# The head flags' load moved from the head of SyncE's queue to behind the first weight gates

## The chip, the cores and the metric

The kernel runs on one core of a Trainium2 chip. The metric is the device time of one execution in microseconds. In the profile PE is TensorE, DVE is VectorE, ACT is ScalarE, POOL is GpSimd and SP is SyncE.

## The reference

Attention with four batches, eight heads, 768 positions and a head size of 64, then a feed-forward layer whose hidden value is the largest of three products:

```
scores = q @ k.T / 8                                   # per batch and head
mask   = causal                     where is_retrieval[head]
         causal & (first 4 keys | last 64 keys)        otherwise
x      = softmax(where(mask, scores, -1e9)) @ v        # -> (3072 rows, 512)
h      = max(x @ w1, x @ w2, x @ w3)                   # 512 -> 768
out    = h @ w_out                                     # 768 -> 512, float32
```

`is_retrieval` holds eight 64-bit flags, 64 bytes as eight pairs of 32-bit words. In the inputs heads 0, 2 and 6 are retrieval heads.

## The kernel before

The kernel is written for a guess of the flags (`GUESS`), and reads the real flags only to test the guess. The flags are loaded into the tile `ir32` (on one partition, 16 words); `compare_flags` (the word `flags` of the order, on POOL) turns them into one number, and a branch at the end runs a general version if the guess was wrong.

All work stands in one order written out by hand, the string `PROGRAM`, whose words are looked up in the table `do`. Each word adds instructions to the queues of its engines, and each engine works through its own queue in that order. What concerns the change is batch 0, whose keys, queries and values are loaded in two halves of 384 positions. The heads are taken as four pairs, `PAIRS`: pair 0 is heads 0 and 2, pair 1 heads 1 and 3, pair 2 heads 4 and 6, pair 3 heads 5 and 7. The loads of half 0 are named here k0 to k3 (tile `ks`), q0 to q3 (tile `qs`), each 192 KB, and va and vb (tile `vs`), the values of heads 0 to 3 and 4 to 7, 384 KB each. The loads of half 1 that follow are k4 to k7 and q4 to q7.

- `load_first` (L310) calls `load_pairs` (L198), one transfer per pair for the keys and one for the queries, at L206. In half 0 all keys go through SP and all queries through ACT (`sc`); in half 1 both go through SP (`ss`).
- Ahead of the order stand k0, q0, k1, q1 and, at L317, the flags on SP. Then `hl 0 2 2 sc` loads k2, k3, q2, q3, and `load_v 0 0 0 4 s` and `load_v 0 0 4 4 s` (L298) load va and vb on SP.
- `cast` (L220) casts a pair to 16 bits, `turnp` transposes it on PE (L238) and copies it out of PSUM to `KQ` (L241). The second line of the order has `turnp 0 0 ad, cast 0 3 pa, ... s0 0 1 1`, and the third `s0 0 0 0, ... turnp 0 3 da, turnp 0 2 da`: pair 3 is cast on POOL (k3) and ACT (q3), and ACT's later work, two exponentials (L638) and the copies of `KQ`, stands behind the cast of q3 in ACT's queue. PE's transposes of pairs 3 and 2, in this order, stand ahead of all later scores (L602, L617).
- `gs i` is a gate: a copy of four bytes of weight matrix i to a scrap tile (`gates`, L286), issued by SP, which must wait for the weights. It keeps SP's later loads back. `w 0`, `w 1` and `w 2` load the weights on POOL (L401).

The queues are also tied together by the transfers' semaphores. In the built program each transfer that SP or ACT issues takes the next of eight semaphores in turn, in one sequence over both queues, and waits until the transfer eight places earlier has landed. The sequence begins q0, k0, q1, k1, flags, k2, k3, q2, va, q3, vb. So va waits for q0, q3 for k0, vb for q1, k4 for k1, and the next for the flags. The order between the two queues is the build's own estimate of when each engine gets to the transfer; within a queue it is the order of the program.

Of the kernel before, what the change touches and what calls it, by code (L numbers as in the profile page):

```python
# [11 lines left out]
INT32 = mybir.dt.int32  # L12
# [141 lines left out]
def fast(ctx, tc, keep, q, k, v, is_retrieval, n_sink, window, moe_w1, moe_w2, moe_w3, moe_w_out, w_t, woutt, out):  # L154
    nc = tc.nc
# [127 lines left out]
    def gate(engine, x):  # L283
        dst = gates[:, next(n_gate)]
        if engine is nc.sync:
            engine.dma_start(out=dst, in_=x)  # L286
        else:
            engine.tensor_copy(out=dst, in_=x)
# [25 lines left out]
    load_first(0, 0, 1)  # L314
    load_first(0, 1, 1)
    ir32 = keep.tile([1, 2 * H], INT32, name="ir32")
    nc.sync.dma_start(out=ir32, in_=is_retrieval.bitcast(INT32).unsqueeze(0))  # L317

    zero = consts.tile([P, 512], FP16, name="zero")
    nc.vector.memset(zero, 0.0)  # L320
# [3 lines left out]
    def idle_work(n):  # L324
# [11 lines left out]
        out=kb[:, 2:4], in_=kb[:, 2:4], compare_op=ALU.is_ge, fill=0.0,  # L336
# [3 lines left out]
        out=kb[:, 3], in_=kb[:, 3], compare_op=ALU.is_gt, fill=0.0,  # L340
# [3 lines left out]
        out=kb[:, 1:5:3], in_=kb[:, 1:5:3], compare_op=ALU.is_gt, fill=0.0,  # L344
# [7 lines left out]
        out=every3, in_=every3, compare_op=ALU.not_equal, fill=1.0,  # L352
# [4 lines left out]
    if n_sink > 0:  # L357
# [4 lines left out]
        out=far, in0=kb[:, 0:5], scalar1=FAR, scalar2=-FAR, op0=ALU.mult, op1=ALU.add  # L362
# [74 lines left out]
    def hidden(b, half, wi, ni, op=None):  # L437
        yy = psum(b, half)
        for ks in range(KS):
            nc.tensor.matmul(  # L440
                yy[:, 0:HALF],
                w_t[wi][:, ks, ni * P : (ni + 1) * P],
                xT[b, half, ks].rearrange("p a t -> p (a t)"),
                start=(ks == 0), stop=(ks == KS - 1),
            )
        if wi == 0:
            acc[b, half, ni] = accp.tile([P, HALF], FP16, tag="acc", name="acc")
            op(out=acc[b, half, ni], in_=yy[:, 0:HALF])  # L448
            return
        if wi == 2:  # L450
            hT[b, half, ni] = htp.tile([P, HALF], FP16, tag=f"hT{ni}", name=f"hT{ni}")
        nc.vector.tensor_tensor(  # L452
            out=acc[b, half, ni] if wi == 1 else hT[b, half, ni],
            in0=yy[:, 0:HALF], in1=acc[b, half, ni], op=ALU.max,
        )
# [65 lines left out]
    def prep_x(b, half, heads, what, op):  # L521
        by_row = b == 0 and half in sorted_halves
        vs = staged_v[b, half] if not by_row else va[0][:, :, half * HB : (half + 1) * HB, 0:D]
        dst = vx[b % 2]
        hs = slice(*map(int, heads.split(":")))
        which = list(range(*hs.indices(H)))
        xs_ = slice(near.index(which[0]), near.index(which[-1]) + 1)
        n = len(which)
        assert near[xs_] == which
        if what == "r":  # L530
            s0 = 2 * half
            k0 = (1, 0)[half]
            op(out=dst[64:P, xs_, s0 : s0 + 2, 0:D], in_=vs[64:P, hs, k0 : k0 + 2])
        else:
            op(
                out=dst[0:64, xs_, :, 0:D],
                in_=vs[0:64, hs, 0:1].to_broadcast([64, n, 4, D]),
            )
# [7 lines left out]
    kx = [[consts.tile([P, 4, P, 2], FP16, name=f"kx{j}{quad}") for quad in range(2)] for j in range(2)]  # L546
# [30 lines left out]
    def far_keys(b, quad, op):  # L577
        src, dst = KQs[b, quad][:, 0], kx[b % 2][quad]
        op(
            out=dst[:, :, 64:P].rearrange("p n c two -> p n (c two)"),  # L580
            in_=src.rearrange("p (n c) two -> p n (c two)", c=P)[:, 1:5, P : 2 * P],
        )
        if n_sink > 0:
            op(
                out=dst[:, :, 0:n_sink].rearrange("p n c two -> p n (c two)"),
                in_=src[:, 0:n_sink].rearrange("p c two -> p (c two)").unsqueeze(1)
                .to_broadcast([P, 4, 2 * n_sink]),
            )
# [54 lines left out]
    def first_masks(hp, u, r, engine):  # L643
        f = "SR"[GUESS[PAIRS[hp][r % 2]]]
        c, pattern = FIRST_KEEP[f, u]
        mask(pts[0, 1, hp, u], r % 2, 1 if r < 2 else 2, c, P, pattern, engine)
# [161 lines left out]
    def reduce_one(out, in_):  # L808
# [9 lines left out]
        k0=lambda hp, u, r, e: first_masks(int(hp), int(u), int(r), engines[e]),  # L818
        s=lambda b, s: scores(int(b), int(s)),
        k=lambda b, s, xy, i, e: masks(int(b), int(s), xy, int(i), engines[e]),  # L820
        f=lambda b, half, wi, ni, *e: hidden(int(b), int(half), int(wi), int(ni), *[ops[x] for x in e]),
# [5 lines left out]
        y=lambda b, half, hs, what, e: prep_x(int(b), int(half), hs, what, ops[e]),  # L827
# [11 lines left out]
        kx0=lambda half, hp, e: far_keys_first(int(half), int(hp), ops[e]),  # L839
        kx=lambda b, quad, e: far_keys(int(b), int(quad), ops[e]),  # L840
        flags=compare_flags,
        check=check_sums,
        verdict=verdict,
        gs=lambda wi: gate(nc.sync, (w_t + [woutt])[int(wi)][0:1, 0, 0:2]),
# [15 lines left out]
def kernel(  # L860
    tc: tile.TileContext,
    q: bass.AP,
    k: bass.AP,
    v: bass.AP,
    is_retrieval: bass.AP,
    n_sink: int,
    window: int,
    moe_w1: bass.AP,
    moe_w2: bass.AP,
    moe_w3: bass.AP,  # L870
    moe_w_out: bass.AP,
    out: bass.AP,
):
    nc = tc.nc
    B, H, S, D = q.shape
    DF, DM = moe_w1.shape[1], out.shape[1]
    with ExitStack() as ctx:
        keep = ctx.enter_context(tc.tile_pool(name="keep", bufs=1))
        w_t = [keep.tile([128, H * D // 128, DF], FP16, name=f"w{wi}t") for wi in range(3)]
        woutt = keep.tile([128, DF // 128, DM], FP16, name="woutt")  # L880
        xs_dram = tc.dram_tile([B * H, S, D], FP16, name="xs_dram")
        n = fast(
            tc, keep, q, k, v, is_retrieval, int(n_sink), int(window),
            moe_w1, moe_w2, moe_w3, moe_w_out, w_t, woutt, out,
        )
        with tc.If(n > 0, preferred_fallthrough_block=True, label="last"):
            general(tc, nc, q, k, v, is_retrieval, int(n_sink), int(window), w_t, woutt, out, xs_dram)
# [164 lines left out]
```

## Time and profile before

| | us |
|---|---|
| time, median of 3 runs | 188.04 (187.54 to 188.54) |
| time of the profiled execution | 187.23 |
| span of its instructions | 185.7 |
| PE busy | 178.3 (96%) |
| DVE busy | 144.7 (78%) |
| ACT busy | 99.4 (54%) |
| POOL busy | 82.8 (45%) |

The span is the time from the first to the last instruction of the profiled execution; 1.5 us of its own time lie around it. Times in views count from the start of the span. A row of the order in time has start, duration, engine, line of the kernel, operation, output and input tile, count, and in brackets the idle time before it with what ended it. An engine's name with a q, such as SPq or ACTq, is its queue of instructions that are not computation; the rows used here are the issue of transfers, not their movement.

### The profile page before, as it was taken

What the parts mean: (1) busy time and instruction counts of PE and PEld (TensorE: products, weight loads), DVE (VectorE), ACT (ScalarE), POOL (GpSimd) and SP (SyncE); (2) the same over time, 40 slices, a digit from 0 to 9 for tenths busy, and PEclk for the clock granted to TensorE, in tenths of its full rate; (3) what the DMA queues carried; (4) which work ended last, traced back from release to release, by engine and by line L of the source; (5) the groups of instructions that cost most, each with busy time, mean ns of one, the idle gap of its engine ahead of it and who ended that gap; (6) DMA issues with size and microseconds to landing.
All of it is one profiled execution on the core that took longest, in us unless ns stands there. A gap on an engine that the chain in (4) does not pass through costs nothing.

```text
span 185.7 us, 4756 instructions
## 1 busy us (share of the span) xinstructions
PE 178.3 (96%) x1863; PEld 105.8 (57%) x1863; DVE 144.7 (78%) x308; ACT 99.4 (54%) x161; POOL 82.8 (45%) x142
## 2 busy tenths in 40 slices
PE   6889999999999999999999999999999999999992
PEld 2455646566656456755555556655755575555551
DVE  3659998989899978888979899755883699474553
ACT  3399998378956648687096336664446301311110
POOL 7498998809793990299057002126313400000000
PEclk9999999999999999999999999999999999999999
DMA  5999999999899999449593301321132013401404
GB/s 166 320 326 287 214 209 210 211 236 216 166 148 158 201 223 201 110 105 218 142 264 84 114 0 56 67 81 56 28 68 109 0 60 64 139 2 56 165 16 166
DMA packets 43009, 26.30 MB, mean 142 GB/s; under 512 B 29798, under 2 KB 38502, under 8 KB 42982
## 3 DMA queue, kind: packets, MB, share of 16 engines
q1 hardware_dynamic: 37558, 17.24, 35.7%
q0 software_dynamic: 4192, 7.87, 23.6%
q10 hardware_dynamic: 1232, 0.85, 1.5%
q8 instruction: 15, 0.25, 0.5%
q14 instruction: 12, 0.10, 0.2%
HBM read 25.17 MB, written 6.29 MB: 169 GB/s over the span
## 4 chain that ended last, share of the span: by engine, by line
PE 85%; DVE 7%; DMA 4%; ACT 2%; issue 0%; DVEq 0%; ACTq 0%
PE yy L440 47%; PE yy L465 15%; PE oacc L726 8%; PE st L683 7%; PE yst L440 3%; DMA qs<-in_q_dram 2%; DVE KQ L241 2%; DMA ks<-in_k_dram 2%; PE yst L465 1%; DVE KQ L275 1%; ACT pt L638 1%; DVE x L733 1%; DVE vx L809 1%; PE st L617 1%; PE vb L514 1%; PE tr L749 1%
## 5 line engine op out<-in xcount | busy, mean ns | idle before, releaser
L380 POOL TENSOR_TENSOR pt<-pt,kb 128x512 f16<-128x512 f16 (+5 forms) x53 | 48.3, 932 | 59.1 <-ACT pt L700 50.2
L700 ACT ACTIVATE pt<-st 128x1024 f16<-128x1024 f32 (+2 forms) x51 | 43.5, 908 | 25.2 <-PE st L683 24.8
L440 PE MATMUL yy<-xT,w2t 128*128 128x384 f16 x184 | 36.2, 326 | 0.0
L440 PE MATMUL yy<-xT,w0t 128*128 128x384 f16 x180 | 34.6, 326 | 0.0
L440 PE MATMUL yy<-xT,w1t 128*128 128x384 f16 x176 | 34.2, 326 | 0.0
L465 PE MATMUL yy<-woutt,hT 128*128 128x512 f16 (+1 forms) x138 | 31.4, 372 | 0.0
L452 DVE TENSOR_TENSOR hT<-yy,acc 128x384 f16<-128x384 f32 x46 | 25.2, 555 | 5.0 <-PE yy L440 3.3
L452 DVE TENSOR_TENSOR acc<-yy,acc 128x384 f16<-128x384 f32 x44 | 23.9, 554 | 5.6 <-PE yy L440 4.2
L275 DVE STREAM_TRANSPOSE KQ<-kq 128x384 f32<-128x384 f32 x24 | 25.3, 1130 | 0.7 <-DMA kq<-in_k_dram 0.7
L440 PEld LDWEIGHTS <-w0t 128*128 128x128 f16 x192 | 18.1, 98 | 12.5 <-issue 0.4
L448 ACT CAST acc<-yy 128x384 f16<-128x384 f32 x27 | 12.9, 492 | 22.6 <-PE yy L440 20.0
L440 PEld LDWEIGHTS <-w1t 128*128 128x128 f16 x192 | 17.8, 98 | 11.9 <-issue 0.6
L440 PEld LDWEIGHTS <-w2t 128*128 128x128 f16 x192 | 17.7, 98 | 11.8 <-issue 0.2
L465 PEld LDWEIGHTS <-hT 128*128 128x128 f16 x150 | 14.4, 98 | 15.3
L726 PEld LDWEIGHTS <-pt 128*128 128x128 f16 x472 | 17.2, 97 | 3.5 <-issue 0.4
L474 ACT COPY ot<-yy 128x512 f32<-128x512 f32 (+1 forms) x14 | 7.9, 566 | 21.0 <-PE yy L465 19.3
L726 PE MATMUL oacc<-va,pt 128*128 128x65 f16 x392 | 18.6, 193 | 0.2 <-DVE pt L380 0.2
L733 DVE TENSOR_TENSOR x<-oacc,sums 128x384 f16<-128x384 f32 x32 | 17.8, 557 | 1.1
L638 ACT ACTIVATE pt<-st 128x1024 f16<-128x1024 f32 (+5 forms) x22 | 15.5, 769 | 0.4 <-PE st L617 0.2
L683 PE MATMUL st<-KQ 32*128 32x128 f16 (+2 forms) x342 | 14.9, 257 | 0.0
L380 DVE TENSOR_TENSOR pt<-pt,kb 128x256 f16<-128x256 f16 (+4 forms) x31 | 12.2, 400 | 2.1 <-ACT pt L700 2.1
L448 DVE CAST acc<-yy 128x384 f16<-128x384 f32 x18 | 10.0, 558 | 3.4 <-PE yy L440 2.9
(119 smaller groups left out, 191.2 us busy)
## 6 DMA issues: line engine op xcount, KB each, us to landing
out_dram<-ot SPq DMA_DIRECT2D x23, 256.0 KB, 2.0
vs<-in_v_dram SPq DMA_DIRECT2D x18, 256.0 KB, 4.9
ks<-in_k_dram SPq DMA_DIRECT2D x8, 192.0 KB, 3.5
kq<-in_k_dram POOLq DMA_DIRECT2D x3, 384.0 KB, 7.5
kq<-in_q_dram POOLq DMA_DIRECT2D x3, 384.0 KB, 9.1
kq<-in_k_dram POOLq DMA_DIRECT2D x3, 288.0 KB, 5.7
kq<-in_q_dram POOLq DMA_DIRECT2D x3, 288.0 KB, 7.1
qs<-in_q_dram ACTq DMA_DIRECT2D x4, 192.0 KB, 4.6
```

What stands on the lines that cost most here:

```text
L275: nc.vector.transpose(out=dst.rearrange("c (p j) -> c j p", j=n)[:, j0:j1], in_=src.rearrange("c (j i) -> c j i", i=R),)
L380: engine.tensor_tensor(out=x, in0=x, in1=of_blocks(kb, pattern, rows), op=ALU.mult)
L440: nc.tensor.matmul(yy[:, 0:HALF], w_t[wi][:, ks, ni * P : (ni + 1) * P], xT[b, half, ks].rearrange("p a t -> p (a t)"), start=(ks == 0), s ...
L448: op(out=acc[b, half, ni], in_=yy[:, 0:HALF])
L452: nc.vector.tensor_tensor(out=acc[b, half, ni] if wi == 1 else hT[b, half, ni], in0=yy[:, 0:HALF], in1=acc[b, half, ni], op=ALU.max,)
L465: nc.tensor.matmul(yo[:, 0:n], hT[b, half, ns][:, tb * P : (tb + 1) * P], woutt[:, ns, c : c + n], start=(ns == 0), stop=(ns == NNB - 1),)
L474: op(out=ot[:, c : c + n], in_=yo[:, 0:n])
L638: nc.scalar.activation(out=pts[0, half, hp, u][:, r0:r1, c0:c1], in_=sts[hp][:, r0:r1, c0:c1], func=AF.Exp, scale=sc,)
L683: nc.tensor.matmul(sts["XY"[g // 2]][:, g % 2, c0 : c0 + n * P], KQ[rows, 0, ki * P : (ki + 1) * P] if kind == "p" else kx[b % 2][quad][ro ...
L700: nc.scalar.activation(out=pts[b, s, xy][:, r0:r1, c0:c1], in_=st[:, r0:r1, c0:c1], func=AF.Exp, scale=sc,)
L726: nc.tensor.matmul(o[:, i, r, 0 : D + 1], at[b, h, kind, ki, qi], vv[:, 0 : D + 1], start=(n == 0), stop=(n == len(todo) - 1), skip_group_ ...
L733: nc.vector.tensor_tensor(out=x, in0=o[:, :, :, 0:D], in1=rc.unsqueeze(3).to_broadcast([P, HB, 2, D]), op=ALU.mult,)
```

## The change

The flags' load no longer stands at L317 between k1 and k2. A new word `ir` issues it from SP, and stands in place of the first of four `gs 0` in a row, behind `gs 1` of the line of `w 1`. Nothing else is moved, and one four-byte transfer is gone.

```
-    "y 0 1 4:5:1 r r, gs 0, gs 0, gs 0, gs 0, k0 0 3 2 d, f 0 0 0 5 a, kx 1 0 a, k0 2 1 0 p",
+    "y 0 1 4:5:1 r r, ir, gs 0, gs 0, gs 0, k0 0 3 2 d, f 0 0 0 5 a, kx 1 0 a, k0 2 1 0 p",
...
     ir32 = keep.tile([1, 2 * H], INT32, name="ir32")
-    nc.sync.dma_start(out=ir32, in_=is_retrieval.bitcast(INT32).unsqueeze(0))
...
         flags=compare_flags,
+        ir=lambda: nc.sync.dma_start(out=ir32, in_=is_retrieval.bitcast(INT32).unsqueeze(0)),
```

## The prediction

> **What bounds the kernel now.** I read the table of stages first: busy time of each engine in stretches of the span (stretch and length, then busy us and count for PE, PEld, DVE, ACT, POOL, then TensorE's granted clock, the DMA engines' share, GB/s).
>
> ```profile
> 4.70:5.40 0.70, 0.70 (x3) 0.23 (x2) 0.00 (x0) 0.00 (x0) 0.24 (x1) 1.00 0.83 211
> 5.40:8.60 3.20, 2.51 (x25) 1.53 (x25) 2.62 (x6) 1.24 (x3) 1.19 (x3) 1.00 1.06 341
> 8.60:13.70 5.10, 4.58 (x51) 2.62 (x50) 2.69 (x8) 4.89 (x9) 5.09 (x15) 1.00 1.10 328
> 13.70:22.20 8.50, 7.72 (x114) 4.84 (x112) 8.20 (x19) 8.09 (x16) 7.60 (x16) 1.00 1.12 255
> 22.20:28.30 6.10, 5.65 (x55) 2.85 (x55) 5.96 (x13) 6.10 (x11) 5.84 (x8) 1.00 1.14 212
> 28.30:60.00 31.70, 31.68 (x415) 20.34 (x416) 29.08 (x58) 21.97 (x37) 21.78 (x39) 1.00 1.04 192
> 60.00:170.00 110.00, 110.00 (x1137) 65.79 (x1135) 86.61 (x187) 54.17 (x85) 37.55 (x52) 1.00 0.43 102
> ```
>
> From 28.3 us on PE has no idle time (31.68 of 31.70, then 110.00 of 110.00). PE's later work is the same before and after, so the end moves by what the moment moves at which PE's unbroken run begins. From 8.6 to 28.3 us ACT, DVE and POOL are nearly full in turn. Only the first 8.6 us wait for data. So the chain of work that ended last comes next; its first pieces (start, duration, what):
>
> ```profile
> 1.05 2.93 DMA ks<-in_k_dram
> ...
> 4.01 4.62 DMA qs<-in_q_dram
> ...
> 8.71 0.51 ACT qn L220
> 9.22 1.20 ACT pt L638 x2
> 10.42 0.75 ACT KQ L241 x2
> 11.17 0.51 ACT pt L638
> ...
> 13.45 0.29 PE tr L238 x3
> ```
>
> The end hangs on one load: q3 is issued when k0 has landed (1.05 + 2.93 = 3.98), lands at 4.01 + 4.62 = 8.63, and ACT's cast of it opens a chain without slack: ACT to 11.68, PE to 13.74, then DVE. The tightness of the later chain is in the table: DVE 8.20 of 8.50 us from 13.7 to 22.2 us, ACT 6.10 of 6.10 to 28.3 us. I therefore pass any shift of q3's landing on to the end one for one.
>
> **What sets q3's landing.** Issues of SP and ACT in order of time, with k2 and k3 in the third row of SP and va in the last:
>
> ```profile
> 1.05 0.98 SPq L206 DMA_DIRECT2D ks<-in_k_dram  x2
> 1.05 1.04 ACTq L206 DMA_DIRECT2D qs<-in_q_dram  x2
> 2.07 0.37 SPq L317 DMA_DIRECT2D ir<-in_is_retrieval_dram  x1
> 2.19 0.42 ACTq L206 DMA_DIRECT2D qs<-in_q_dram  x1
> 2.49 0.90 SPq L206 DMA_DIRECT2D ks<-in_k_dram  x2
> 4.01 0.37 ACTq L206 DMA_DIRECT2D qs<-in_q_dram  x1
> 4.30 0.37 SPq L298 DMA_DIRECT2D vs<-in_v_dram  x1
> ```
>
> The landings are read from the casts that wait for them: q1 on DVE, q2 and k3 on POOL, k2, k4 and q4 on DVE, and q3 on ACT.
>
> ```profile
> 5.43 0.55 DVE L220 CAST qn<-qs 128x384 f16<-128x384 f32 x1 [1.15 <-DMA qs<-in_q_dram]
> 7.29 0.51 POOL L220 CAST qn<-qs 128x384 f16<-128x384 f32 x1 [1.64 <-DMA qs<-in_q_dram]
> 7.46 0.55 DVE L220 CAST kn<-ks 128x384 f16<-128x384 f32 x1 [0.56 <-DMA ks<-in_k_dram]
> 8.17 0.51 POOL L220 CAST kn<-ks 128x384 f16<-128x384 f32 x1 [0.37 <-DMA ks<-in_k_dram]
> 8.71 0.51 ACT L220 CAST qn<-qs 128x384 f16<-128x384 f32 x1 [0.99 <-DMA qs<-in_q_dram]
> 11.77 0.55 DVE L220 CAST kn<-ks 128x384 f16<-128x384 f32 x1 [0.99 <-DMA ks<-in_k_dram]
> 12.93 0.55 DVE L220 CAST qn<-qs 128x384 f16<-128x384 f32 x1 [0.61 <-DMA qs<-in_q_dram]
> ```
>
> Two readings. First, the loads come in the order of issue over both queues, one after the other: q2 (issued 2.19) at 7.29, k2 (2.49) at 7.46, k3 at 8.17, q3 (4.01) at 8.71, and behind it va, vb and k4 by 11.77. From k4 to q4 two transfers of 192 KB land in 12.93 - 11.77 = 1.16 us, so 0.58 us each, and 1.16 us for 384 KB. k3 was issued after q2 and q3 after k3; ACT's queue, though it had q3 from 4.01, did not bring it before k3. Second, q1 to k2 takes 7.46 - 5.43 = 2.03 us for two transfers that cost 1.16: 0.87 us are lost around the place of the flags. The table of stages shows the same hole: 211 GB/s between 4.7 and 5.4 us against 341 after it, a loss of 0.70 x (341 - 211) / 341 = 0.27 us on the mean of the 16 DMA engines. Landings show more than the mean, since a load has landed with its slowest part.
>
> **The change part by part.**
>
> *The flags leave the head of the queue.* SP issues k2 and k3 0.42 us earlier (2.49 to 2.07), since 0.37 us of issue and a gap go. That alone buys nothing: k2's data move after q1's. What may go is the hole. Its price lies between 0 (a stall at the first touch of a new stretch of memory or after any pause would stay, with k2 or q2 in its place) and -0.87 us (the flags cause all of it). The mean of engines says -0.27. I take -0.45, between the two rows, nearer to the mean of engines; both ends stay for the range. A loss from this removal alone I exclude, since it takes work out of the stream.
>
> *The sequence of semaphores moves up by one place.* With the flags out, the first eight are q0, k0, q1, k1, k2, k3 and then va and q2 in some order. So va, ninth before, becomes seventh or eighth and waits for nobody; q3 stays behind it, ninth or tenth, and still waits for q0 or k0. SP's waits for queries before it issued va and vb are this row of its queue (waited for, us in total, times, longest):
>
> ```profile
> SPq L298 <- DMA qs<-in_q_dram: 1.6, 2, 0.9
> ```
>
> So va is issued right behind k3, at 2.07 + 0.90 = 2.97 us, where before it came at 4.30; q3 comes at 4.01 (behind k0) or 4.30 (behind q0). The 384 KB of va now stand ahead of q3 in the stream: +1.16 us for q3. The lower end is 0, if the two queues share the engines at that point; the upper end is vb too, another 1.16 us, if vb gets the wait for k0 (3.98) and q3 that for q0. I take +1.16: SP reaches vb in the build's estimate one place after va, just before ACT reaches q3, so vb waits for q0 (it goes out at about 4.30) and q3 for k0 (4.01), as before.
>
> *What is behind them.* k2, q2 and k3 land no later, but the order has pair 3 first on PE, and q3 is its last part; ACT waits for it with two ready exponentials queued behind its cast, PE with its transposes behind those. va lands about 1.2 us earlier, which only POOL's casts of it use. k4 to q7 lie behind the same bytes as before; they gain the hole's part at most, and DVE's casts of them are not what DVE waits for at 13.76 us:
>
> ```profile
> 13.76 0.56 DVE L241 COPY KQ<-tr 128x384 f16<-128x384 f16 x1 [0.27 <-PE tr L238]
> ```
>
> *The other end.* Behind the gate on w1 the flags take a gate's place:
>
> ```profile
> 29.35 0.72 SPq L286 DMA_DIRECT2D gates<-w1t  x1
> 30.18 2.37 SPq L286 DMA_DIRECT2D gates<-w0t  x4
> ```
>
> The uses of w2, of the flags and of the values of batch 1 are in the views of these tiles (shortest, median and longest duration in ns, first and last start in us):
>
> ```profile
> L440 PE MATMUL yy<-xT,w2t x184: 323/326/337, 37.9 to 177.9; 128*128 128x384 f16 x184
> L401 POOL DMA_DIRECT2D w2t<-in_moe_w_dram x1: 829/829/829, 26.8 to 26.8; - x1
> DMA to landing us min/median/max: 10.1/10.1/10.1
> ```
>
> ```profile
> L767 POOL TENSOR_SCALAR none<-ir x1: 279/279/279, 46.1 to 46.1; 1x16 f32<-1x16 int32 x1
> L487 DVE CAST va<-vs x5: 349/350/900, 47.4 to 119.7; 128x384 f16<-128x384 f32 x5
> ```
>
> A gate costs 2.37 / 4 = 0.59 us of SP, the flags 0.37, so the values of batch 1 go out 0.2 us earlier, for a use at 47.4 us: nothing. They run beside w2, issued at 26.8 and landed after 10.1 us at 36.9, used at 37.9: 1.0 us of cover against at most 0.2. The flags are needed at 46.1 and land some 14 us before: nothing. From here on every transfer keeps its distance of eight to the one that it waits for. Price 0; without w2's cover it would be at most 0.2 us.
>
> **Sum.** -0.45 + 1.16 = +0.7 us on the profiled execution: 187.23 (185.7 of span and 1.5 around) to 187.9. The median of the runs lies 0.8 us higher, at 188.04; against it the forecast is 188.04 + 0.7 = 188.7. What a measurement of this kernel can tell from no change is about 0.5%, 0.94 us. The forecast's own range, with -0.87 and 0 for the hole, is +0.3 to +1.2, 188.3 to 189.2.
>
> **The rivals.**
>
> *Both value loads pass q3.* It is decided by which of vb and q3 gets the earlier place. Then q3 stands 2.32 us later: +2.32 - 0.45 = +1.9, 189.9. Against it: SP comes to vb before ACT comes to q3 in the sequence as I read it. For it: before, va and q3 already stood side by side.
>
> *va does not hold q3 up.* If both queues hold descriptors at once and the engines take turns, q3 runs at half speed beside va: 0.58 us more instead of 1.16, so +0.58 - 0.45 = +0.1, 188.2: no change. Against it are the landings above, where q3, four us in its queue, came behind k3. For it: these rows show one order of four loads of ACT, and none of them behind a transfer as large as va. [...]
>
> *The early data come earlier.* If the build puts q3 ahead of va, q3 is among the first eight and goes out at 2.19 + 0.42 = 2.61 us without a wait, va behind it as before, and the hole's loss is all that changes: -0.45, at best -0.87, 187.6 to 187.2. It decides from the point where q3 is eighth. Against it: va moves up with SP's queue, q3 does not move.
>
> **How the numbers follow.** The forecast 0.55 (of which 0.19 above +0.94, where the hole stays), both loads 0.15, turns 0.15, earlier 0.15 (0.09 of it faster by over 0.5%, with what the measurement adds, and 0.06 no change; of the turns 0.02 are faster likewise). Faster 0.11, same 0.36 + 0.13 + 0.06 = 0.55, slower 0.19 + 0.15 = 0.34. The range runs from 187.3, with most of the hole gone at no price, to 190.0, just over both loads ahead of q3.
>
> **What would show it.** Right: va's issue at about 3.0 us and q3's still at 4.0 to 4.3; the cast of q3 on ACT at about 9.4 us (8.9 to 9.9); ACT's idle time before it grown from 0.99 us; 13.76 and the start of PE's unbroken run moved alike. The hole: GB/s between 4.7 and 5.4 us near 341, and 1.2 us between the casts of q1 and the later of k2 and q2 of pair 2. Wrong: the cast of q3 at or before 8.71, or the end not moved by as much as that cast.

## The result and the profile after

The kernel became slower. Its median is 191.28 us (190.73 to 191.51, six runs) beside 188.13 us (187.54 to 188.54, six runs) for the kernel before in the same session: a ratio of 1.0168, 95% interval 1.0143 to 1.0193, or +3.15 us. The forecast was 188.7 us with a range up to 190.0. The profiled execution took 191.51 us, with a span of 190.0 us.

From here "after" is the changed kernel; its lines after L317 stand one lower than in the kernel before, so the scores at L617 are now at L616. First the issues of SP and of ACT in order of time, k0 to k3 being the first row of SP:

```profile
1.05 2.00 SPq L206 DMA_DIRECT2D ks<-in_k_dram  x4
3.10 1.13 SPq L298 DMA_DIRECT2D vs<-in_v_dram  x2
6.61 0.88 SPq L206 DMA_DIRECT2D ks<-in_k_dram  x2
1.05 1.04 ACTq L206 DMA_DIRECT2D qs<-in_q_dram  x2
4.18 0.37 ACTq L206 DMA_DIRECT2D qs<-in_q_dram  x1
```

Both value loads are out by 3.10 + 1.13 = 4.23 us, and q3 is issued at 4.18, behind the start of both. In the built program q3 now has the ninth place and vb the tenth: q3 waits for q0 and vb for k0. SP's wait ahead of its two value loads is now this one (waited for, us in total, times, longest), where before it was two waits for queries:

```profile
SPq L298 <- DMA ks<-in_k_dram: 0.3, 1, 0.3
```

This is the order that the rival "both value loads pass q3" named. The chain of work that ended last (start, duration, what) shows what q3 pays for it:

```profile
1.05 3.11 DMA qs<-in_q_dram
4.18 7.46 DMA qs<-in_q_dram
...
11.72 0.52 ACT qn L220
...
12.29 1.06 PE tr L238 x9
...
17.33 0.29 PE tr L238 x3
...
32.19 1.39 PE oacc L725 x39
```

q0 lands at 1.05 + 3.11 = 4.16 and releases q3, which takes 7.46 us to land where it took 4.62. ACT's cast of q3 starts at 11.72 instead of 8.71 (+3.01). PE's transposes for half 1 start at 17.33 instead of 13.45 (+3.88), and PE's unbroken run at 32.19 instead of 28.29 (+3.90; both are the row of 39 `oacc` matmuls in the chain). The row of the kernel before is this one:

```profile
28.29 1.39 PE oacc L726 x39
```

From there the shift stays: PE's last matmul starts 3.9 us later, and the span grew by 4.3 us. The other 0.4 came behind PE's last matmul: from its start to the end this execution took 4.2 us, the profiled execution before 3.8. The medians differ by only 3.15 because the execution profiled before lay 0.9 us under its median and the one after 0.2 over.

So 3.01 us came with q3, and another 0.9 between its cast and the transposes for half 1. The table of stages shows where (columns as in the table of the prediction; the last two rows are stretches that I chose around the wait for q3; other rows are left out):

```profile
4.70:5.40 0.70, 0.70 (x3) 0.23 (x2) 0.04 (x1) 0.00 (x0) 0.00 (x0) 1.00 0.76 200
5.40:8.60 3.20, 2.12 (x19) 0.94 (x17) 1.98 (x5) 1.42 (x3) 0.51 (x2) 1.00 1.02 329
9.00:12.41 3.41, 1.10 (x13) 0.66 (x12) 1.15 (x4) 0.69 (x2) 3.41 (x11) 1.00 1.10 326
12.40:15.80 3.40, 3.40 (x23) 1.55 (x21) 1.70 (x5) 2.64 (x6) 2.69 (x7) 0.50 0.87 251
```

Three readings. The hole between 4.7 and 5.4 us is still there, 200 GB/s without the flags against 211 with them. From 12.4 to 15.8 us PE is busy all the time, but TensorE's granted clock is 0.50; before, every stage had 1.00. And in the 3.41 us ahead of that PE had been busy for 1.10 us only, because it waited for q3. All six executions of the changed kernel paid this: one stretch of 3.4 us at half of the clock lowers the mean over 190 us by 3.4 x 0.5 / 190 = 0.009, and their mean granted clocks are 0.990 and 0.991. Of 65 executions of the kernel before in the sessions below, two were under 0.995 (0.989 and 0.991, with 189.25 and 189.24 us). The wait, and behind it three transposes in 0.53 us, in order of time, and then three transposes in the kernel before, at the full clock:

```profile
12.29 0.42 PE L238 MATMUL tr<-ident,qn 128*128 128x128 f16 x3 [2.27 <-ACT qn L220]
12.50 0.53 PE L238 MATMUL tr<-ident,kn 128*128 128x128 f16 x3
```

```profile
9.46 0.33 PE L238 MATMUL tr<-ident,kn 128*128 128x128 f16 x3
```

The casts of q1 and q3, as quoted in the prediction for the kernel before:

```profile
6.62 0.55 DVE L220 CAST qn<-qs 128x384 f16<-128x384 f32 x1 [1.88 <-DMA qs<-in_q_dram]
11.72 0.51 ACT L220 CAST qn<-qs 128x384 f16<-128x384 f32 x1 [3.18 <-DMA qs<-in_q_dram]
```

The first is q1's, 1.19 us later than before (5.43). That is this execution's; where the same order of loads was run again below, q1's cast began at 5.50 to 5.63.

### The profile page after: what moved, and what is told of

Its sections match the earlier page's. It is cut to its first block, busy times and chain, and to the rows that moved or that the text cites. A ratio compares the mean times of both kernels' runs of the same rounds, so it can differ in the third digit from the quotient of the medians.

```text
span 190.0 us, 4755 instructions
## 1 busy us (share of the span) xinstructions
PE 180.0 (95%) x1863; PEld 106.0 (56%) x1863; DVE 145.2 (76%) x308; ACT 99.7 (52%) x161; POOL 82.8 (44%) x142
## 4 chain that ended last, share of the span: by engine, by line
PE 85%; DVE 7%; DMA 6%; issue 1%; ACT 0%; DVEq 0%; ACTq 0%
PE yy L439 46%; PE yy L464 15%; PE oacc L725 7%; PE st L682 7%; DMA qs<-in_q_dram 6%; PE yst L439 3%; DVE KQ L241 2%; PE st L601 1%; PE st L616 1%; PE yst L464 1%; DVE KQ L275 1%; DVE x L732 1%; DVE vx L808 1%; PE vb L513 1%; PE tr L748 1%; PE tr L238 1%
## 5 line engine op out<-in xcount | busy, mean ns | idle before, releaser
L275 DVE STREAM_TRANSPOSE KQ<-kq 128x384 f32<-128x384 f32 x24 | 25.3, 1133 | 0.0
L682 PEld LDWEIGHTS <-KQ 32*128 32x128 f16 x342 | 8.8, 92 | 6.5 <-issue 5.7
```

Source lines behind the costliest of these rows:

```text
L275: nc.vector.transpose(out=dst.rearrange("c (p j) -> c j p", j=n)[:, j0:j1], in_=src.rearrange("c (j i) -> c j i", i=R),)
L682: nc.tensor.matmul(sts["XY"[g // 2]][:, g % 2, c0 : c0 + n * P], KQ[rows, 0, ki * P : (ki + 1) * P] if kind == "p" else kx[b % 2][quad][ro ...
```

## The experiments

The theory after this reading: one transfer fewer ahead of them moves the sequence of eight semaphores up by one place; so vb no longer waits for q1 and q3 stands behind 768 KB of values; what is left is TensorE's clock, halved after PE's wait. The rivals: the flags' late place costs something (SP's queue, the lost gate); or the time comes from the values being early, not from q3 being late; or the clock has no part in it. Ratios are to the kernel before in the same session, with 95% intervals.

**A second copy of the flags at the old place.** After, with one more load of the flags, which nothing reads, between k1 and k2:

```
+    irx = keep.tile([1, 2 * H], INT32, name="irx")
+    nc.sync.dma_start(out=irx, in_=is_retrieval.bitcast(INT32).unsqueeze(0))
```

> The changed kernel, with a second load of the flags, into a tile that nobody reads, in the old place between k1 and k2. Theory (the sequence of eight semaphores moved up by one place, so that va and vb are issued ahead of q3): the sequence is as before again, q3 is cast on ACT at about 8.7 us, TensorE's clock stays at 1.00, 188.1 us, within 0.5 us of the kernel before. Rival (the flags at their new place behind the weights, or the missing gate, cost the time): it stays at 191.3 us.

Measured: 188.20 us, ratio 1.0000 (0.9979 to 1.0020). The whole loss is gone, though the real flags are still loaded late and the gate is still missing. The cast of q3 in order of time, in this kernel:

```profile
8.78 0.51 ACT L220 CAST qn<-qs 128x384 f16<-128x384 f32 x1 [1.00 <-DMA qs<-in_q_dram]
```

It starts 0.07 us from its place before, and the clock is 1.00 throughout (0.995 to 1.000 in all ten executions). So a 64-byte transfer at the head is worth 3.1 us here as a place holder in the sequence, and the new place of the flags costs nothing that can be measured.

**The flags right behind the values.** After, with the word `ir` moved from the gates to behind the load of vb:

```
-    "load_v 0 0 4 4 s, turnp 0 0 ad, ...
+    "load_v 0 0 4 4 s, ir, turnp 0 0 ad, ...
-    "y 0 1 4:5:1 r r, ir, gs 0, ...
+    "y 0 1 4:5:1 r r, gs 0, ...
```

> The changed kernel, with the flags loaded on SP right behind vb instead of behind the gate on w1 (that gate's place is left empty). Theory (only the first eleven places of the sequence count): va and vb still pass q3, so it is as the changed kernel: q3 cast at 11 to 11.8 us, the clock halved behind it, 190.7 to 191.5 us. Rival (the late place of the flags, or the gates, cost the time): back at 188.1.

Measured: 191.17 us, ratio 1.0153 (1.0126 to 1.0179), as after. The flags' own place does not matter as long as they are behind q3. In this kernel's order of time, and its stages:

```profile
11.45 0.51 ACT L220 CAST qn<-qs 128x384 f16<-128x384 f32 x1 [3.48 <-DMA qs<-in_q_dram]
12.02 0.50 PE L238 MATMUL tr<-ident,qn 128*128 128x128 f16 x3 [2.57 <-ACT qn L220]
32.63 0.20 PE L725 MATMUL oacc<-va,pt 128*128 128x65 f16 x1 [0.24 <-DVE pt L379]
7.11:10.53 3.42, 2.08 (x22) 1.16 (x19) 2.09 (x5) 0.87 (x3) 2.44 (x8) 1.00 1.10 342
10.53:13.95 3.42, 1.93 (x14) 1.32 (x15) 1.07 (x4) 2.50 (x6) 2.40 (x8) 0.50 1.07 316
13.95:17.36 3.41, 3.41 (x19) 0.98 (x17) 0.63 (x2) 2.09 (x3) 3.39 (x6) 0.50 1.00 285
```

In this execution, the slowest of four, the clock was 0.50 for two stretches of 3.4 us, twice as long as in the one after; the other three had mean clocks of 0.989 to 0.991, about one such stretch, and took 190.34 to 191.27 us. The first of the two stretches began while PE still waited, and the wait left PE busy for only 1.93 us of it. +2.74 us on q3's cast became 32.63 - 28.29 = +4.34 on PE's run, 1.6 us more.

**One value load ahead of q3 instead of two.** After, with an unread copy of the flags on SP between va and vb, so that vb waits for q1 as before, while va stays ahead of q3:

```
-    "... cast 0 2 dp, load_v 0 0 0 4 s",
+    "... cast 0 2 dp, load_v 0 0 0 4 s, irx",
```

> The changed kernel, with a second load of the flags, into a tile that nobody reads, on SP between va and vb: vb now waits for q1 and is issued behind q3, va still ahead of it. Theory (each value load ahead of q3 costs q3 its whole duration, 1.2 us): q3 is cast at 10.5 us instead of 11.72, and the time is 189.9 us with the clock at 1.00, 190.5 with the clock halved for a while. Rival (the two queues share the engines, and q3 is late for another reason): the cast stays within 0.4 us of 11.7 and the time near 191.3.

Measured: 189.26 us, the median of nine runs (a tenth took 194.71), ratio 1.0064 (1.0030 to 1.0098), a little under what was expected. In order of time, with the stages around the wait:

```profile
3.10 0.47 SPq L298 DMA_DIRECT2D vs<-in_v_dram  x1
4.36 0.37 ACTq L206 DMA_DIRECT2D qs<-in_q_dram  x1
5.55 0.39 SPq L298 DMA_DIRECT2D vs<-in_v_dram  x1
10.30 0.51 ACT L220 CAST qn<-qs 128x384 f16<-128x384 f32 x1 [2.74 <-DMA qs<-in_q_dram]
10.86 0.34 PE L238 MATMUL tr<-ident,qn 128*128 128x128 f16 x3 [1.38 <-ACT qn L220]
30.62 0.20 PE L726 MATMUL oacc<-va,pt 128*128 128x65 f16 x1 [0.23 <-DVE pt L380]
7.84:11.25 3.41, 1.63 (x19) 0.87 (x17) 1.25 (x4) 0.95 (x3) 2.87 (x10) 1.00 1.08 330
11.30:14.60 3.30, 3.30 (x19) 0.99 (x16) 1.69 (x5) 2.78 (x5) 3.29 (x8) 0.50 1.11 326
```

q3's cast is 1.59 us later than before and PE's run 2.33. This is the kernel that the forecast described: one load of 384 KB ahead of q3. In this execution the forecast's sum for this case was short too, by the hole that did not go and by the 0.74 us between cast and run, in which the clock stood at 0.50 again, here after a wait of only 1.38 us. But the clock did not fall each time. Three of the nine had a mean clock of 0.991 (189.58, 189.69 and 190.89 us), five 0.999 or 1.000 (188.28 to 189.26, median 188.79), one 0.997 (190.44). By the ratio the kernel lost 1.2 us, about the forecast's 1.16 for one value load with nothing for the hole.

**PE kept busy during the wait.** After, with 10 and then 12 matmuls of 512 columns on zeros in place of one, ahead of the transposes that wait for q3:

```
-    "s0 0 0 0, hl 1 0 2 ss, idle 1, turnp 0 3 da, ...
+    "s0 0 0 0, hl 1 0 2 ss, idle 10, turnp 0 3 da, ...    (then: idle 12)
```

> The changed kernel, with 10 idle products of zeros instead of 1 in PE's queue ahead of the transposes of pair 3, where PE waits for q3. Theory (the wait of 2.27 us on PE is what halves TensorE's granted clock for 3.4 us behind it, and this costs 0.9 us on the path): q3's cast stays at 11.7 us, the clock stays at 1.00 from 11.7 to 17.7 us, the time falls by about 0.9 us to 190.4. Rival (the lower clock costs nothing, because ACT sets the pace there): 191.3 us with the clock at 1.00. Second rival (the clock falls whatever PE does): clock 0.7 as in the changed kernel and 191.3 us.

> The changed kernel with 12 idle products of zeros instead of 1 in front of the transposes of pair 3 (10 kept the clock at 1.00 and brought the maximum-of-products steps of PE forward by 1.05 us up to 125 us, which was lost again to a late transposing transfer there). Theory (the halved clock costs 0.9 us, and the late transfer in the run with 10 was chance): clock 1.00, the steps forward by about 0.9 us to the end, 190.4 us. Rival (a gain at the start is always taken back behind 125 us by SP's transposing transfers): the same wait near 127 us, 191.2 us.

Measured with 10: 191.22 us, ratio 1.0165 (1.0115 to 1.0216, four runs), no gain. With 12: 189.99 us, ratio 1.0120 (1.0092 to 1.0147, six runs), 1.3 us under after by the medians and 0.9 by the ratios. The two intervals just touch, but five of the six runs lie at 189.8 to 190.4, below all six of after (190.7 to 191.5). The cast and the start of PE's run, with 12 in order of time and its stage:

```profile
11.28 0.51 ACT L220 CAST qn<-qs 128x384 f16<-128x384 f32 x1 [3.72 <-DMA qs<-in_q_dram]
30.85 0.20 PE L725 MATMUL oacc<-va,pt 128*128 128x65 f16 x1 [0.23 <-DVE pt L379]
12.40:15.80 3.40, 2.88 (x30) 1.39 (x28) 1.70 (x5) 3.31 (x6) 3.39 (x9) 1.00 1.01 296
```

and with 10, with the first wait of PE behind the start of its run:

```profile
11.09 0.51 ACT L220 CAST qn<-qs 128x384 f16<-128x384 f32 x1 [3.61 <-DMA qs<-in_q_dram]
30.68 0.20 PE L725 MATMUL oacc<-va,pt 128*128 128x65 f16 x1 [0.26 <-DVE pt L379]
127.74 0.32 PE L439 MATMUL yy<-xT,w0t 128*128 128x384 f16 x1 [0.74 <-DMA xT<-x]
```

In both the clock is 1.00 throughout, and what q3 is late is passed on exactly: +2.57 on the cast and 30.85 - 28.29 = +2.56 on the run with 12, +2.38 and +2.39 with 10. From the cast to the run it is 19.6 us in both, as in the kernel before (28.29 - 8.71), beside 20.3 and 20.5 us with one stretch at half of the clock (one value load, after) and 21.2 with two (flags behind the values). So the early values cost nothing beyond making q3 late. The expected time of the first was missed all the same: its profiled execution lost 0.74 us to a transposing transfer at 127.7 us that came late, and 0.18 to another at 143.9. Whether that befell its other three timed runs as well, no view of them can say; one of them also had a mean clock of 0.990 (192.33 us). With 12 matmuls all six runs kept 0.997 to 1.000, and the gain came through to the end. In the profiled executions PE's run starts 32.19 - 30.85 = 1.34 us earlier with 12 than after: 11.72 - 11.28 = 0.44 is q3 itself, and 0.90 the clock.

**All eight head loads without a wait.** After, with pairs 2 and 3 issued ahead of the order, so that q3 is eighth and both values stand behind it:

```
+    load_first(0, 2, 2)
-    "idle 11, hl 0 2 2 sc, cast 0 1 pd, ...
+    "idle 11, cast 0 1 pd, ...
```

> The changed kernel, with the loads of pairs 2 and 3 ahead of the order, so that ACT issues q2 and q3 before its warm-up exponential; no flags at the head. Theory: q0 to q3 and k0 to k3 are the first eight of the sequence, va and vb come behind them; q3 is cast at 8.3 to 8.8 us and the time is 187.5 to 188.3 us. Rival (the data engines run worse when the flags are not at the head, whatever the order): q3 is cast at 10 us or later, 189.5 us or more.

Measured: 188.79 us, ratio 1.0048 (1.0018 to 1.0078). In order of time, with the first two stages:

```profile
1.05 2.08 ACTq L206 DMA_DIRECT2D qs<-in_q_dram  x4
4.30 0.92 SPq L298 DMA_DIRECT2D vs<-in_v_dram  x2
8.98 0.51 ACT L220 CAST qn<-qs 128x384 f16<-128x384 f32 x1 [1.61 <-DMA qs<-in_q_dram]
4.70:5.40 0.70, 0.70 (x4) 0.16 (x2) 0.00 (x0) 0.00 (x0) 0.27 (x1) 1.00 0.88 202
5.40:8.60 3.20, 2.04 (x21) 1.21 (x21) 2.46 (x5) 1.30 (x3) 0.75 (x2) 1.00 0.96 300
```

q3 was issued by 3.13 instead of from 4.01 on, and landed no earlier: in this order too the eight loads together need till about 8.9 us, and the hole of 202 GB/s is there without the flags. There was nothing to gain at the head by the issue alone. The expected time was missed: this kernel is 0.7 us slower than the kernel before, of which the cast explains 0.27. Two of the ten runs had mean clocks of 0.988 and 0.991; where the rest went stays open.

**Another order instead of q3 first.** Four kernels looked for a version that beats the kernel before. The first takes that kernel, loads pair 3 ahead of pair 2 and casts it first; the second also issues the loads of half 1 ahead of the values; the third is the first with half 1's loads in the order k4, q4, k5, q5; the fourth has only this last change.

```
-            for h in range(0, 2 * n, 2):
+            for h in (2, 0) if (half, hp, n) == (0, 2, 2) else range(0, 2 * n, 2):
...
-    "idle 11, hl 0 2 2 sc, cast 0 1 pd, turnp 0 1 aa, cast 0 0 dd, cast 0 2 dp, load_v 0 0 0 4 s",
-    "load_v 0 0 4 4 s, turnp 0 0 ad, cast 0 3 pa, cleark 0 p, ...
+    "idle 11, hl 0 2 2 sc, cast 0 1 pd, turnp 0 1 aa, cast 0 0 dd, load_v 0 0 0 4 s",
+    "load_v 0 0 4 4 s, turnp 0 0 ad, cast 0 3 pa, cast 0 2 dp, cleark 0 p, ...
```

> The kernel before (flags at the head), with k3, q3 loaded ahead of k2, q2 and pair 3 cast ahead of pair 2. Theory (loads land in the order of issue over both queues; q3 lands one and a half places earlier, q2 takes q3's old place): q3's cast at about 7.5 us, q2's at 8.7, and since the fourth queries of half 1, cast at 12.9 us, hold PE next, 0.1 to 0.7 us faster than before: 187.4 to 188.0. Rival (q2's transposes then hold PE as q3's did): 188.1.

```
-    "... cast 0 0 dd, load_v 0 0 0 4 s",
-    "load_v 0 0 4 4 s, turnp 0 0 ad, ...
-    "s0 0 0 0, hl 1 0 2 ss, idle 1, ...
+    "... cast 0 0 dd, hl 1 0 2 ss",
+    "load_v 0 0 0 4 s, load_v 0 0 4 4 s, turnp 0 0 ad, ...
+    "s0 0 0 0, idle 1, ...
```

> As the kernel with pair 3 first (flags at the head), and with the first four loads of half 1 (k4, k5, q4, q5) issued ahead of va and vb. Theory: these four land 2.3 us earlier, va and vb 2.3 us later (about 13.4 us); q2 stands behind k4 at most. If PE's next wait was q4, the chain from 13.4 us starts up to 1 us earlier and the time falls to 187.2; if the values are then late for their casts on POOL at 10.5 us, POOL's queue is held up by 2 us and the time rises to 189 to 190. I expect the second.

```
+        hs = range(0, 2 * n, 2)
+        todo = [(i, h) for i in range(2) for h in hs]
+        if (half, hp) == (1, 0):
+            todo = [(i, h) for h in hs for i in range(2)]
+        for i, h in todo:
...
```

> The kernel before, with pair 3 loaded and cast ahead of pair 2, and with the first four loads of half 1 issued as k4, q4, k5, q5 in the place of k4, k5, q4, q5. With pair 3 first the PE waited for q4's cast at 13.6 us, so there the bound had only moved from q3 to q4. If a load lands in the order of issue, q4 lands about one load of 192 KB (some 0.6 us) earlier and the first oacc step begins up to 0.5 us earlier: 187.6 to 187.9 us beside 188.1 of before. Rival: the first eight loads land by about 8.7 us whatever their order and something else (k5, or the values) holds the PE at the same place: 188.1 to 188.4 us.

> The kernel before, with nothing changed but the order k4, q4, k5, q5 of half 1's first four loads. There q3's chain holds the PE until 13.4 us, and q4 is in by then: no change is expected, 187.9 to 188.3 us. Rival: k5, now one load later, holds the PE up, and the time goes up by as much as 0.6 us to 188.7 us.

Measured, in this order: 188.34 us, 1.0005 (0.9981 to 1.0028); 190.89 us, 1.0163 (1.0136 to 1.0189, four runs); 188.29 us, 1.0039 (1.0015 to 1.0064); 187.83 us, 1.0009 (0.9986 to 1.0033). None is faster: the gains expected of the first and the third did not come, the third is 0.4% slower, and the fourth was expected to change nothing. The second is slow as expected: POOL's cast of the first values started at 12.44 us instead of 10.5, and behind it PE had 1.19 us without work in the 4.00 us from 13.70 on, where the chain of work goes from POOL's `kx` to PE's scores at 14.88. The execution with that view took 189.07 us at a clock of 1.00; the other three had 0.991 and took 190.54 to 191.45. The third shows why nothing was gained: q4 came early as expected, and PE's run began at 27.95, 0.34 us earlier, but DVE then waited for the keys of the next batch, which POOL had issued some 11 us earlier. The row is DVE's in order of time, first in the kernel before and then in the third of these kernels (whose L281 is L275):

```profile
31.33 2.08 DVE L275 STREAM_TRANSPOSE KQ<-kq 128x384 f32<-128x384 f32 x2 [0.74 <-DMA kq<-in_k_dram]
```

```profile
27.95 0.20 PE L732 MATMUL oacc<-va,pt 128*128 128x65 f16 x1 [0.21 <-DVE pt L386]
31.85 2.08 DVE L281 STREAM_TRANSPOSE KQ<-kq 128x384 f32<-128x384 f32 x2 [1.60 <-DMA kq<-in_k_dram]
34.38 2.11 PE L446 MATMUL yy<-xT,w1t 128*128 128x384 f16 x12 [0.37 <-DVE acc L458]
```

That load ends DVE's wait at 31.3 to 31.9 us in both, and PE, which before had no idle time there, waits 0.37 us for DVE. In these executions an earlier q3 or q4 is worth nothing while this load lands where it does.

## Why the prediction was wrong, point by point

**What bounds the kernel: right, in one direction.** q3's landing sets the start of PE's unbroken run, and a later landing is passed on one for one: +2.38 became +2.39 and +2.57 became +2.56 where the clock stayed at 1.00. Downwards it does not hold, as the early q4 showed. The forecast's gain for the hole would probably have been lost there, had the hole gone alone.

**The failed step: the order of vb and q3 in the sequence.** The forecast said that SP reaches vb just before ACT reaches q3, so that vb waits for q0 and q3 for k0. The built program had it the other way round: q3 ninth, behind q0 (landed 4.16), vb tenth, behind k0. A wait for k0 held vb up for 0.3 us only (SP's row of two issues, 1.13 us from 3.10, has that gap in it), so vb was out before q3: the earlier place brought q3 the later release. The chance of 0.15 for this rival was too low: the text itself noted that va and q3 stood side by side before.

**The term for the hole: mis-sized.** -0.45 us was taken and nothing came. Between 4.7 and 5.4 us the six kernels without a small load at the head moved 200 to 265 GB/s, four of the six with one 188 to 276 (flags or a copy of them at the head: before 211, the second copy 188, pair 3 first 276, values last 222). From q1's cast to the later of those of k2 and q2 it was 2.00 and 2.05 us with ten and twelve matmuls, beside 2.03 before. That was the stated upper end, 0.

**The term for the values: about the right price, one load short.** 1.16 us each was forecast, 2.32 for both. 768 KB (0.79 MB) at the 329 GB/s of the stages are 2.4 us, and the runs of this order had q3's cast 2.38 (ten matmuls), 2.57 (twelve) and 2.74 (flags behind the values) later. The remaining 0.3 to 0.6 us in the execution profiled after go with its late q1; that they come from it is not shown. With va alone it was 1.59, 0.4 more than forecast; why stays open. Had the two queues taken turns, as the rival "va does not hold q3 up" has it, only as much of va and vb as q3 itself holds, 192 KB or an estimated 0.6 us at 329 GB/s, would have passed ahead of it, and its cast would have started by about 8.71 + 0.6 = 9.3 us. In the four executions of this order it started at 11.09 to 11.72. The packets that the two queues moved in the kernel after show where the time went (q1 is SP's queue, q10 ACT's; packets, MB, share of the engines' time), first from 7 to 8 us and then from 8 to 11:

```profile
q1 hardware_dynamic: 463, 0.35, 102.0%
q10 hardware_dynamic: 17, 0.01, 3.4%
```

```profile
q1 hardware_dynamic: 1113, 0.82, 88.1%
q10 hardware_dynamic: 273, 0.20, 21.8%
```

q3 is the last of ACT's four loads, a quarter of their 1088 packets. It had been issued at 4.18, but from 7 to 8 us SP's queue moved nearly alone, and q3's packets followed from 8 us on, side by side with SP's. So the two queues shared the engines while q3 moved, but its packets began some 4 us behind its issue; what held them back stays open. The prediction's reading "one after the other" holds for the landings, not for the packets.

**The missing term: TensorE's clock.** The forecast held every stage at the 1.00 of the profile before. The wait for q3 took PE's busy time to 1.10 us in 3.41, and the next stretch ran at 0.50 for 3.4 us, which cost 3.90 - 3.01 = 0.9 us. With twelve matmuls on zeros in the wait the clock stayed at 1.00 and the 0.9 us were gone. The forecast named "the end not moved by as much as that cast" as a sign of being wrong, and this is that sign. The slow stretch was 3.4 us long here, and twice that in the execution with the flags behind the values (10.53 to 17.36 us). What went with it was a wait of PE of 2.27 us here and of 2.57 us there, and in the execution with one value load one of 1.38 us, with 1.63 us busy in the 3.41 us ahead of the slow stretch.

**The other end: right.** The flags behind the gate cost nothing that can be measured: 188.20 us with a place holder at the head and the flags still late.

**Sum.** On the profiled executions: q3 +3.01 (2.4 for 768 KB, the rest this execution's), the clock +0.9, 0.4 behind PE's last matmul: +4.3 of span. The rival's price of +1.9 was 2.32 less a hole that stayed; with 0 for the hole and 0.9 for the clock it would have been +3.2, beside +3.15 measured between the medians.

## What to carry to other kernels

Where transfers take semaphores in turn from a small ring, as here from eight, a tiny load at the head is also a place holder (64 bytes were worth 3.1 us): taking it out moves every later wait by one place, and the sequence of the built program, over all queues, has to be written down before and after, since neighbours from two queues can swap. Ask of each large transfer that is freed from a wait what it now overtakes; here a load that nobody needed yet belonged behind the one that the chain waited for. And when a wait of PE grows (here waits of 1.38 to 2.57 us went with a clock of 0.50 for 3.3 us or more), look at the granted clock of the next stretch, and price it, before passing the shift on one for one.

## What the hardware showed that was not expected

- In three profiled executions TensorE's clock was halved around waits of 2.27, 2.57 and 1.38 us, with 1.10 us (after), 2.08 us (flags behind the values) and 1.63 us (one value load) of PE work in the 3.4 us ahead of the slow stretch. With 3.00 us busy of 3.10 while q3 was awaited it stayed at 1.00, in the kernel with twelve matmuls on zeros:

```profile
8.60:11.70 3.10, 3.00 (x19) 1.34 (x15) 0.27 (x2) 0.42 (x2) 1.60 (x6) 1.00 1.10 331
```

Whether a limit lies between these, and where, was not looked for. The profiled execution with all eight head loads issued first kept 1.00 with 2.04 us busy of 3.20, and six of the nine runs with one value load ahead of q3 had a mean clock of 0.997 or more: the same order of work does not always lose the clock. What decides it stays open.

- The hole near 5 us (188 to 276 GB/s from 4.7 to 5.4 us, against 300 to 345 from 5.4 to 8.6, in ten kernels) does not come from the 64-byte load, since it is there with and without one; what causes it stays open. It was not tried with fewer or smaller loads.
- Issuing q3 about 1 us earlier, without a wait, did not bring it earlier (cast at 8.98 against 8.71): in this kernel the order and the bytes of the loads counted, not the time of issue.
